# Operand sums of a two-layer network made earlier, stored in DRAM and loaded back

## The chip, the cores and the metric

The kernel runs on one core of a Trainium2 chip. The metric is the device time of one launch in microseconds (us). Before the change the median of three runs is 1302.47 us (1299.16 to 1303.53).

## The reference

Three layers follow each other. Attention through 32 packed queries per head gives x with 4608 tokens of 512 channels. A mixture of experts sends each token to one of 8 experts. A dense network with two matrices ends it:

```python
def _moe2_ref(x, w_in, w_out):        # x 4608 x 512, w_in 512 x 2048, w_out 2048 x 512
    h = x @ w_in
    g = h * (1.0 / (1.0 + np.exp(-h)))
    return (g @ w_out).astype(np.float32)
```

All is float32. The change concerns this last network, and the place in the expert stage where its weights are converted.

## The kernel before

The program has three parts: attention (0 to 280 us), the experts, called the middle stage here (`experts`, 280 to 516 us), and the dense network (`ffn`, 516 us to the end). The part `ffn` again has two phases.

**Seven products in place of eight.** Both matrix products cut each operand into 2 by 2 corners and use seven corner products (a Strassen scheme, `terms`): A11 B11, A12 B21, S4 B22, A22 T4, S1 T1, S2 T2, S3 T3. S1 to S4 are sums of activation corners, T1 to T4 sums of weight corners. Every operand is held as a high part (rounded to `fp32r`, a ScalarE cast) and a low part (source minus high part, a subtraction); three matmuls make one precise product.

**Middle stage.** `conv` turns 32 blocks of the 64-bit weights into float32 with six VectorE instructions each, and `conv_store` writes them to `wf_d`.

**Phase 1** computes silu(x @ w_in) in 40 calls of `group(z, g)`: z is one of five blocks of tokens (the last, z = 4, is half as wide), g one of eight blocks of W_in. The first eight groups have z = 0; the other 32 follow the list `order`, and position i below is an index into it. A group is seven times six matmuls (`Pm`, lines 844 to 846). It drains its PSUM banks a, b, c, d with VectorE sums and ScalarE silus into a ring of tiles `cs`, stored to `c_d[z]` as four corners 0 to 3 (C11, C12, C21, C22). The seventh product of a group is issued inside the next one. Other work (weight operands, activation sums, corners of W_out) is queued with `later` and issued in four places of a group (`hook`), each with a budget in nanoseconds. `operand(g, x)` builds the 14 parts of W_in block g into one of four tiles TT[0..3]; blocks 4 to 7 are built twice. `corner_steps` and `build4` split W_out; blocks 5 to 7 go to `v_d` and are loaded back by `slice_load` into TT[1..3], since those tiles still hold W_in until phase 1 ends.

**Phase 2** works through 18 units (z, 128 columns of each corner), four for z = 0 to 3 and two for z = 4. A unit has seven products in the order 1, 7, 6, 2, 5, 3, 4, each of eight pairs of matmuls (lines 1081 and 1082). For each product `split` casts 128x1024 values on ScalarE (line 1059) and subtracts on VectorE, two products ahead. `drain` empties PSUM; GpSimd adds two halves (`both`) and SyncE writes the output. `load_unit` fetches the four corners of the next unit. Their sums are made on GpSimd, four instructions of 128x1024 a unit: E1 = C21 + C22 and C21 = C11 - C21 (`early_sums`, in `split` of product 5), C11 = E1 - C11 (after product 1's split), C12 = C12 - C11 (after product 2's):

```python
        if i == 1:
            tt(POOL, c11, E1, c11, ALU.subtract)
        elif i == 2:
            tt(POOL, c12, c12, c11, ALU.subtract)
        elif i == 5 and 0 < u < len(units) - 1:
            early_sums(u + 1)
```

Every engine runs its instructions in program order. SyncE (SP) issues all DMAs here, also in order: an issue that waits holds up those behind it. `tt` records every VectorE and GpSimd sum of `ffn` under line 837.

## Time and profile before

| | |
|---|---|
| median of 3 runs | 1302.47 us |
| profiled execution | 1308.87 us, of which the span of its instructions is 1307.1 us |
| TensorE (PE) busy | 1210.1 us, 93% of the span |
| VectorE (DVE) busy | 831.9 us, 64% |
| ScalarE (ACT) busy | 542.1 us, 41% |
| GpSimd (POOL) busy | 477.0 us, 36% |
| moved by DMA | 235.71 MB |
| mean granted TensorE clock | 0.983 |

TensorE is the busiest engine. The stretches in which it isn't busy are short and spread over the second half of the span, so the profile is read by stage: 280 to 516 us the middle stage, 516 to 867 us phase 1 as far as its last three narrow groups, 867 to 932 us the passage to phase 2, 932 to 1286 us the units of phase 2.

### The profile page before, as it was taken

Reading aid. Unit: us, or ns where it says so; the run is one execution under the profiler, and the core shown is the slowest. Engines: PE = TensorE matmul, PEld = TensorE weight load, DVE = VectorE, ACT = ScalarE, POOL = GpSimd, SP = SyncE. Lnnn points to the kernel's source line nnn. Section 1 sums busy time; section 2 is a strip of 40 time slices with the busy share of each in tenths; the row PEclk is TensorE's granted clock in tenths of the full one; section 3 lists DMA queues with packets and bytes.
Section 4 is the critical chain, followed back from the end, with each engine's and each line's share of the span. In section 5 each row is a group of like instructions: output and inputs, shape, how many; then the busy total and the mean of one; then the engine's idle time right before and its main releaser. Section 6 shows DMA issues by size and latency. Waiting matters only on the chain. (4 is left out here: it accounts for less than half of the span.)

```text
span 1307.1 us, 23467 instructions
## 1 busy us (share of the span) xinstructions
PE 1210.1 (93%) x9008; PEld 1042.3 (80%) x9009; DVE 831.9 (64%) x1323; ACT 542.1 (41%) x925; POOL 477.0 (36%) x430
## 2 busy tenths in 40 slices
PE   6999989999999999999999999997899999999997
PEld 4777668999999999777788778876677787778876
DVE  2566557678886765785563566644667666666664
ACT  2666652334233314654453445543333333333342
POOL 2233210000000001761252313422876767676865
PEclk9999999999999999999999999997999999999999
DMA  6897738567976564634346544788435353525351
GB/s 190 243 256 219 239 103 296 195 219 254 333 235 233 165 209 129 209 133 161 135 153 220 191 129 160 254 294 287 125 97 145 97 145 97 145 81 157 85 160 34
DMA packets 237686, 235.71 MB, mean 180 GB/s; under 512 B 34168, under 2 KB 185208, under 8 KB 237440
## 3 DMA queue, kind: packets, MB, share of 16 engines
q1 hardware_dynamic: 231040, 229.44, 55.9%
q10 hardware_dynamic: 6528, 4.72, 1.2%
q8 instruction: 72, 1.18, 0.4%
q14 instruction: 46, 0.38, 0.1%
HBM read 155.60 MB, written 78.51 MB: 179 GB/s over the span
## 5 line engine op out<-in xcount | busy, mean ns | idle before, releaser
L837 DVE TENSOR_TENSOR x<-p,x 128x512 f32<-128x512 f32 (+1 forms) x171 | 109.2, 649 | 94.1 <-POOL raw L837 40.8
L876 ACT ACTIVATE x<-x 128x512 f32<-128x512 f32 (+1 forms) x114 | 67.9, 598 | 144.9 <-DVE x L837 133.3
L1081 PE MATMUL p<-x,e 128*128 128x512 f32 x315 | 118.2, 402 | 2.7 <-DMA x<-v_d 2.7
L601 PE MATMUL ps<-hkm,w2s 128*128 128x288 f32 x384 | 114.5, 298 | 0.9 <-DVE yb L612 0.9
L603 PE MATMUL ps<-hkm,w2s 128*128 128x288 f32 x384 | 113.5, 296 | 1.4 <-DVE w2s L574 1.4
L305 POOL TENSOR_TENSOR cu<-co,co 128x256 f32<-128x256 f32 x1 | 0.7, 729 | 284.7 <-PEq L682 284.7
L602 PE MATMUL ps<-hqm,w2s 128*128 128x288 f32 x320 | 94.2, 294 | 0.0
L1082 PE MATMUL p<-x,x 128*128 128x256 f32 x320 | 91.9, 287 | 0.0
L837 DVE TENSOR_TENSOR x<-p,y 128x512 f32<-128x512 f32 (+1 forms) x75 | 50.1, 668 | 44.5 <-PE p L846 40.4
L601 PEld LDWEIGHTS ps<-hkm,w2s 128*128 128x128 f32 x384 | 72.1, 188 | 7.6 <-DVE hqm L537 5.0
L1081 PEld LDWEIGHTS p<-x,e 128*128 128x128 f32 x315 | 60.0, 191 | 17.0 <-DMA x<-v_d 3.1
L603 PEld LDWEIGHTS ps<-hkm,w2s 128*128 128x128 f32 x384 | 72.0, 188 | 1.9 <-DVE w2s L574 1.8
L837 POOL TENSOR_TENSOR raw<-x 128x256 f32<-128x256 f32 x72 | 69.6, 981 | 8.3 <-DVE x L837 6.0
L528 PE MATMUL ps<-at,mh 128*128 128x288 f32 x224 | 66.8, 298 | 3.0 <-PEq L682 3.0
L837 POOL TENSOR_TENSOR raww1c<-raww1c 128x1024 f32<-128x1024 f32 x18 | 56.9, 3160 | 30.4 <-issue 29.7
L530 PE MATMUL ps<-at,mh 128*128 128x288 f32 x224 | 66.8, 298 | 0.0
L529 PE MATMUL ps<-at,mh 128*128 128x288 f32 x224 | 66.7, 298 | 0.0
L1059 ACT CAST e<-rawe 128x1024 fp32r<-128x1024 f32 x27 | 28.3, 1049 | 91.7 <-POOL rawe L837 91.7
L837 POOL TENSOR_TENSOR rawe<-rawe 128x1024 f32<-128x1024 f32 x18 | 57.8, 3213 | 20.8 <-issue 20.1
L1082 PEld LDWEIGHTS p<-x,x 128*128 128x128 f32 x320 | 62.7, 196 | 0.0
L533 ACT ACTIVATE hkm<-ps 128x576 fp32r<-128x576 f32 x42 | 27.4, 653 | 84.1 <-PE ps L530 83.9
L573 ACT CAST w2s<-w2c 128x1024 fp32r<-128x1024 f32 x32 | 33.8, 1055 | 66.4 <-PE ps L602 42.0
(423 smaller groups left out, 3895.4 us busy)
## 6 DMA issues: line engine op xcount, KB each, us to landing
c_d<-x SPq DMA_DIRECT2D x128, 256.0 KB, 2.0
raww1c<-c_d SPq DMA_DIRECT2D x36, 512.0 KB, 7.2
rawe<-c_d SPq DMA_DIRECT2D x36, 512.0 KB, 6.4
w1c<-in_moe_w_dram SPq DMA_DIRECT2D x32, 512.0 KB, 7.1
w2c<-in_moe_w_dram SPq DMA_DIRECT2D x32, 512.0 KB, 6.6
y_d<-yb SPq DMA_DIRECT2D x36, 288.0 KB, 4.5
raw<-wf_d SPq DMA_DIRECT2D x38, 256.0 KB, 3.3
raw<-y_d SPq DMA_DIRECT2D x36, 256.0 KB, 4.6
```

Source lines behind the costliest of these rows:

```text
L528: PE.matmul(out=a[:, i, 0:H2], lhsT=mh[0][:, t, f], rhs=at[0][:, t, n], start=t == 0, stop=False)
L529: PE.matmul(out=a[:, i, 0:H2], lhsT=mh[0][:, t, f], rhs=at[1][:, t, n], start=False, stop=False)
L530: PE.matmul(out=a[:, i, 0:H2], lhsT=mh[1][:, t, f], rhs=at[0][:, t, n], start=False, stop=t == 1)
L573: ACT.copy(out=h, in_=w2c[c % 2])
L601: PE.matmul(out=a[:, i, 0:H2], lhsT=h[:, k, :], rhs=hT(0, k, n), start=k == 0, stop=False)
L602: PE.matmul(out=a[:, i, 0:H2], lhsT=h[:, k, :], rhs=hT(1, k, n), start=False, stop=False)
L603: PE.matmul(out=a[:, i, 0:H2], lhsT=l[:, k, :], rhs=hT(0, k, n), start=False, stop=k == 7)
L837: eng.tensor_tensor(out=o, in0=x, in1=y, op=op)
L876: ACT.activation(out=y, in_=x, func=ACTF.Silu)
L1059: ACT.copy(out=h, in_=src)
L1081: PE.matmul(out=o, lhsT=h[:, g], rhs=x, start=first and n == 0, stop=False, skip_group_check=True)
L1082: PE.matmul(out=o[:, 256:512], lhsT=l[:, g], rhs=x[:, 0:256], start=False, stop=n == G - 1, skip_group_check=True)
```

## The change

- Middle stage: after every second conversion GpSimd makes T1 to T4 of that block with four subtractions of 128x256, and SP stores them to `u_d` (16 blocks: eight of W_in, eight of W_out). `ffn` loads them into `x4` where it made them before, on GpSimd.
- Phase 1: the low parts that GpSimd made go to VectorE. For z above 0, a group also makes E1 = C21 + C22 and C21 = C11 - C21 with two VectorE instructions, and stores five tiles in place of four. The ring `cs` gets a seventh tile.
- W_in blocks 4 to 7 are stored to `t_d` after their first use (1.835 MB each, i = 0 to 3) and loaded back after i = 20, 21, 24 and 25, in place of a second build.
- Passage: the four tiles of W_out for `build4` are loaded at i = 27, before `load_unit(0)`; the fourth goes to `x4`. `build4` and `early_sums(0)` run on VectorE alone. `slice_load` of blocks 6 and 7 (TT[2], TT[3]) is one DMA each; block 5 comes last, and the first two products take it after the other seven.
- Phase 2: C11 and C12 sums on VectorE. For z above 0, `early_sums` is a load of E1. GpSimd keeps only `both`.

```diff
@@ experts: conv
+        if 7 < i < 16 or i >= 24:
...
+            for q, x, y in ((t1, b12, b11), (t2, b22, t1), (t3, b22, b12), (t4, b21, t2)):
+                POOL.tensor_tensor(out=q, in0=x, in1=y, op=ALU.subtract)
+            for n in range(2):
+                SP.dma_start(out=u_d[i - 8 if i < 16 else i - 16][:, 512 * n:512 * n + 512], in_=four[n])
@@ ffn: group
+                def f():
+                    e1 = ring()
+                    tt(DVE, e1, c21, kept[22])
+                    store(4, e1)
+                    tt(DVE, c21, kept[11], c21, ALU.subtract)
+                    store(2, c21)
+                return f
@@ ffn
+    def t_load(g, x):
+        held[g] = x
+        SP.dma_start(out=TT[x][:, 0:3584].bitcast(F32), in_=t_d[g].bitcast(F32))
@@ ffn: split, early_sums
         if i == 1:
-            tt(POOL, c11, E1, c11, ALU.subtract)
+            tt(DVE, c11, E1, c11, ALU.subtract)
         elif i == 2:
-            tt(POOL, c12, c12, c11, ALU.subtract)
+            tt(DVE, c12, c12, c11, ALU.subtract)
         elif i == 5 and 0 < u < len(units) - 1:
             early_sums(u + 1)
 
     def early_sums(u):
+        if units[u][0]:
+            load_unit(u, (4,))
+            return
         c11, c12, c21, c22 = raws[u % 2]
-        tt(POOL, E1, c21, c22)
-        tt(POOL, c21, c11, c21, ALU.subtract)
+        tt(DVE, E1, c21, c22)
+        tt(DVE, c21, c11, c21, ALU.subtract)
@@ ffn: the list order, from i = 16
-             (3, 0), (3, 1), (3, 2), (4, 0), (3, 3), (4, 1), (3, 4), ...
+             (3, 0), (3, 1), (3, 2), (4, 0), (4, 1), (3, 3), (3, 4), ...
+    next_t = {19: (4, 0), 20: (5, 1), 23: (6, 2), 24: (7, 3)}
...
+        if i < 4:
+            t_store(4 + i)
...
+        if i - 1 in next_t:
+            t_load(*next_t[i - 1])
@@ ffn: the first products of phase 2
+        if s < 2:
+            product(s, (0, 1, 2, 3, 4, 6, 7))
+            if s:
+                for x in range(2):
+                    product(x, (5,))
+                    drain(x)
```

VectorE in phase 2, from the end of one unit with z = 3 into the next, before (raww1c and rawe hold the corners of alternate units, x_7157 is E1, e, at, x_9864 and x_9995 are low parts, p are PSUM banks):

```order
L837 TENSOR_TENSOR at_135<-rawe_10060,at_134 128x1024
L837 TENSOR_TENSOR x_7158<-p_7162,x_7158 128x512
L837 TENSOR_TENSOR x_9864<-rawe_10060,e_3365 128x1024
L837 TENSOR_TENSOR x_7158<-p_7161,y_3367 128x512
L837 TENSOR_TENSOR x_9995<-rawe_10060,x_9995 128x1024
L837 TENSOR_TENSOR e_3365<-rawe_10060,e_3365 128x1024
L837 TENSOR_TENSOR at_135<-x_7157,at_134 128x1024
L837 TENSOR_TENSOR y_3367<-p_7164,y_3366 128x512
L837 TENSOR_TENSOR x_9864<-rawe_10060,e_3365 128x1024
L837 TENSOR_TENSOR x_9995<-rawe_10060,x_9995 128x1024
L837 TENSOR_TENSOR x_7158<-p_7164,y_3366 128x512
L837 TENSOR_TENSOR x_7158<-p_7165,x_7158 128x512
```

The same part of VectorE's program after the change (x_7259 is E1):

```order
L849 TENSOR_TENSOR at_141<-rawe_10108,at_140 128x1024
L849 TENSOR_TENSOR rawe_10108<-x_7259,rawe_10108 128x1024
L849 TENSOR_TENSOR x_7260<-p_7264,x_7260 128x512
L849 TENSOR_TENSOR x_9910<-rawe_10108,e_3371 128x1024
L849 TENSOR_TENSOR x_7260<-p_7263,y_3373 128x512
L849 TENSOR_TENSOR x_10044<-rawe_10108,x_10044 128x1024
L849 TENSOR_TENSOR e_3371<-rawe_10108,e_3371 128x1024
L849 TENSOR_TENSOR rawe_10108<-rawe_10108 128x1024
L849 TENSOR_TENSOR at_141<-x_7259,at_140 128x1024
L849 TENSOR_TENSOR y_3373<-p_7266,y_3372 128x512
L849 TENSOR_TENSOR x_9910<-rawe_10108,e_3371 128x1024
L849 TENSOR_TENSOR x_10044<-rawe_10108,x_10044 128x1024
```

Two instructions are new in a unit, the second and the eighth row: C11 and C12, which were on GpSimd.

SP in phase 2, one unit with z = 2, before (c_d_76 to 79 are the four corners):

```order
L1032 DMA raww1c<-c_d_76 128x8x128
L1032 DMA raww1c<-c_d_79 128x8x128
L1032 DMA raww1c<-c_d_78 128x8x128
L1032 DMA raww1c<-c_d_77 128x8x128
L1127 DMA out_dram<-raw 128x512 x2
```

And after (c_d_79 to 82 are the four corners, c_d_83 is E1):

```order
L1077 DMA raww1c<-c_d_79 128x8x128
L1077 DMA raww1c<-c_d_81 128x8x128
L1077 DMA raww1c<-c_d_82 128x8x128
L1077 DMA raww1c<-c_d_80 128x8x128
L1077 DMA x_7259<-c_d_83 128x8x128
L1175 DMA out_dram<-raw 128x512 x2
```

A fifth load stands behind the four, into the one tile of E1, and ahead of the two writes of the output.

## Rows read from the trace of the kernel before

**Rows 1.** Stretches: length, busy us of PE, PEld, DVE, ACT, POOL; PEclk, DMA, GB/s
```profile
280.00:516.00 236.00, 231.86 (x1822) 223.59 (x1821) 179.28 (x282) 80.30 (x114) 5.44 (x6) 0.99 0.68 222
340.00:360.00 20.00, 20.00 (x153) 20.00 (x152) 17.69 (x30) 6.28 (x10) 0.00 (x0) 1.00 0.93 318
516.00:867.00 351.00, 335.92 (x1559) 276.13 (x1558) 217.58 (x325) 167.88 (x344) 130.49 (x146) 1.00 0.52 181
867.00:932.00 65.00, 47.39 (x265) 41.56 (x265) 30.36 (x37) 25.43 (x41) 29.71 (x15) 0.87 0.74 234
932.00:1286.00 354.00, 329.38 (x1808) 280.96 (x1807) 225.93 (x194) 127.64 (x145) 253.90 (x130) 0.98 0.44 119
```
**Rows 2.** ScalarE in time: start, us, operation; one copy a group (L903), a unit (L1098)
```profile
661.42 0.59 ACT L903 COPY y<-p 128x512 f32<-128x512 f32 x1
670.94 0.59 ACT L903 COPY x<-p 128x512 f32<-128x512 f32 x1
...
931.58 0.58 ACT L1098 COPY y<-p 128x512 f32<-128x512 f32 x1
...
1285.66 0.58 ACT L1098 COPY y<-p 128x512 f32<-128x512 f32 x1
```
**Rows 3.** Chain of waits through one unit of phase 2: start, us, what
```profile
1023.40 7.08 DMA raww1c<-c_d
...
1030.64 2.79 POOL x L837
...
1038.18 2.35 POOL raww1c L837
...
1043.25 1.77 DVE x L837
...
1045.74 6.80 DMA rawe<-c_d
```
**Rows 4.** TensorE in phase 2, two matmuls eight pairs apart
```profile
957.19 0.39 PE L1081 MATMUL p<-x,e 128*128 128x512 f32 x1
...
959.97 0.39 PE L1081 MATMUL p<-x,x 128*128 128x512 f32 x1
```
**Rows 5.** VectorE in phase 2: start, us, operation, idle time before it
```profile
1023.90 1.22 DVE L837 TENSOR_TENSOR at<-x,at 128x1024 fp32r<-128x1024 f32 x1
1025.59 0.69 DVE L837 TENSOR_TENSOR y<-p,y 128x512 f32<-128x512 f32 x1 [0.47 <-PE p L1082]
...
1038.12 3.48 DVE L837 TENSOR_TENSOR at<-raww1c,at 128x1024 fp32r<-128x1024 f32 x1
```
**Rows 6.** GpSimd beside the last of these
```profile
1038.14 2.38 POOL L837 TENSOR_TENSOR raww1c<-x,raww1c 128x1024 f32<-128x1024 f32 x1
```
**Rows 7.** SP's issues of one unit's loads
```profile
1022.05 4.71 SPq L1032 DMA_DIRECT2D raww1c<-c_d  x4
```
**Rows 8.** Landing of the loads of phase 2: KB each, median us to landing
```profile
raww1c<-c_d SPq DMA_DIRECT2D x28, 512.0 KB, 7.2
```
**Rows 9.** TensorE in the passage, with idle time before and its releaser
```profile
888.32 0.58 PE L844 MATMUL p<-e,t 128*128 128x256 f32 x1 [7.40 <-DVE raw L837]
...
902.01 0.80 PE L1081 MATMUL p<-x,e 128*128 128x512 f32 x1 [2.73 <-DMA x<-v_d]
```
**Rows 10.** Chain of waits in the passage
```profile
871.65 7.48 DMA c_d<-x
...
879.15 4.80 DMA x<-wf_d
```
**Rows 11.** VectorE in the passage, a narrow drain
```profile
874.18 0.42 DVE L837 TENSOR_TENSOR x<-p,x 128x256 f32<-128x256 f32 x1
```
**Rows 12.** The page: a GpSimd subtraction of 128x256 (mean in ns after the busy time)
```profile
L305 POOL TENSOR_TENSOR cu<-co,co 128x256 f32<-128x256 f32 x1 | 0.7, 729 | 284.7 <-PEq L682 284.7
```
**Rows 13.** TensorE in the passage, narrow group: two matmuls eight trios apart
```profile
870.09 0.28 PE L844 MATMUL p<-e,t 128*128 128x256 f32 x1
...
872.97 0.28 PE L844 MATMUL p<-e,t 128*128 128x256 f32 x1
```

More of the change, by code (lines that the diff above doesn't have):

```diff
@@ L206, in build @@
             P = [ps.tile([128, 2, 512], F32, name=f"ps{i}") for i in range(4)]
[L207 removed]
+            experts(tc, s1, sums, R, P, first, ident, a2_d, y_d, g_d, pp_d, w1, w2, win, wout, wf_d, u_d)
         s2.close()
         with ExitStack() as s1:
[L210 removed]
+            ffn(tc, s1, sums, y_d, wf_d, t_d, c_d, u_d, v_d, out)
 class Early:
@@ L316, in both @@
                 x()
-        return [lambda: both(*steps, his[0], his[1]), *[lambda i=i: both(*his[i + 2:i + 3], los[i]) for i in range(6)]]
+        return [lambda: both(*(steps if fresh else ()), his[0], his[1]), *[lambda i=i: both(*his[i + 2:i + 3], los[i]) for i in range(6)]]
 class Fixed:
@@ L557, in experts @@
     raw = [T([128, 512], f"raw{i}") for i in range(4)]
+    four = sums.y3
     turn = [0]
@@ L807, in experts, with ffn @@
                 conv_store(x)
-def ffn(tc, st, sums, y_d, wf_d, c_d, u_d, v_d, out):
+def ffn(tc, st, sums, y_d, wf_d, t_d, c_d, u_d, v_d, out):
     nc = tc.nc
@@ L972, in ffn, with both_k, get @@
+    def both_k(z, now, then):
+        r0, r1 = {}, {}
+        def get(r, k, i):
+            r[i] = fetch(z, k, i)
+        for i in (3, 2, 0, 1):
+            get(r0, 0, i)
+        dead = {6: 3, 7: 2, 9: 0, 10: 1}
+        later(now, *steps(z, 0, r0, {m: (lambda i=i: get(r1, 1, i)) for m, i in dead.items()}))
+        later(then, *steps(z, 1, r1))
     win = dict(zip((1, 9), sums.next))
+    w = wf_d.bitcast(F32)
+    tmp = [x4[:, 256 * i:256 * i + 256] for i in range(4)]
+    ow = {}
     def win_load(g):
-        win[g], win[g + 8] = w_raw(g), w_raw(g + 8)
@@ L1135, in ffn @@
     X = [x1[i // 4][:, 512 * (i % 4):512 * (i % 4) + 512] for i in range(8)]
-    load(1, 0, X[0:4])
+    for i in range(4):
+        fetch(1, 0, i, X[i])
     todo = [*steps(1, 0, X[0:4]), *steps(1, 1, X[4:8])]
@@ L1142, in ffn @@
         if g == 2:
-            load(1, 1, X[4:8])
+            for i in range(4):
+                fetch(1, 1, i, X[4 + i])
         if g in (5, 6):
@@ new lines, in ffn @@
+            later(now + 4, *operand(i - 4, i - 4))
+        if i == 11:
+            both_k(3, now + 5, now + 10)
+        if i == 16:
+            k = [[fetch(4, k, j) for j in range(2)] for k in range(2)]
+            k = [{0: x[:, 0:256], 1: y[:, 0:256], 2: x[:, 256:512], 3: y[:, 256:512]} for x, y in k]
+            later(now + 4, *steps(4, 0, k[0]), *steps(4, 1, k[1]))
+        if i in (19, 21, 23, 25):
+            n = (i - 19) // 2
+            flush()
+            o_load(4 + n if n else 0)
+            later(now + 3, *corner_steps(4 + n if n else 0, slices(n - 1) if n else slice0))
@@ L1254, in ffn @@
+        if i == 27:
+            flush()
+            for x, y in (("B11", at[0]), ("T3", at[1]), ("T2", half(b, 3)), ("B21", x4)):
+                staged(x, y)
         if i == 28:
-            flush()
             raws[0] = quarters("w1c")
-            for x, y in (("B11", at[0]), ("T2", x4), ("T3", at[1])):
-                later(now + 1, (0, lambda x=x, y=y: staged(x, y)))
-            later(now + 1, (0, lambda: load_unit(0)))
+            load_unit(0)
         if i == 29:
-            later(now, (0, small))
@@ L1262, in ffn @@
-            later(now + 1, (0, lambda: staged("B21", x5[:, 0:1024])), b4("B11", DVE), b4("T2", DVE), b4("T3", POOL))
+            later(now + 1, (0, small))
+            later(now + 1, b4("B11"), b4("B21"), b4("T3"))
         if i == 30:
-            later(now, (0, lambda: early_sums(0)))
-            later(now + 1, (0, lambda: slice_load(1)), b4("B21", DVE), (0, lambda: split(0)))
+            later(now, (0, lambda: slice_load(1)))
+            later(now, b4("T2"), (0, lambda: early_sums(0)), (0, lambda: split(0)))
```

202 lines of the change are left out of this document (95 added, 107 removed).

## Prediction

> **What bounds the kernel now.** I read the busy time by stretch first, to see where TensorE isn't busy, then for each such stretch what it waits for. The middle stage has almost nothing to give: TensorE is busy 231.86 of 236 us [rows 1]. Phase 1 has 351 - 335.92 = 15 us of idle TensorE, the passage 65 - 47.39 = 17.6 us at a mean granted clock of 0.87, phase 2 354 - 329.38 = 24.6 us [rows 1]. Idle time is not all: in phase 2 the copy that opens a unit comes 16 times between 931.58 and 1285.66 us, so a unit takes 354.08 / 16 = 22.13 us [rows 2], while TensorE alone needs less: eight pairs take 959.97 - 957.19 = 2.78 us, seven products 19.5 us [rows 4]. So each unit lasts 2.6 us longer than its matmuls.
>
> The chain of waits says why [rows 3]. It goes through one unit in a loop that TensorE is hardly in: the load of the next corners (7.08 us), GpSimd's sums one behind the other (2.79 us for E1 and more until 1040.5), the last splits on VectorE (1.77 us), and then the tiles are free and the next load starts at 1045.74, 22.3 us after the one before. GpSimd is busy 253.90 of 354 us there [rows 1]. VectorE is drawn in: a low part of 128x1024 takes 1.22 us alone and 3.48 us beside a GpSimd sum of 2.38 us [rows 5, 6]. What bounds phase 2 is GpSimd's chain, not TensorE.
>
> **Phase 2, units 1 to 17.** For z above 0 the four GpSimd sums leave the loop: two are made in phase 1, two go to VectorE. VectorE's work in a unit is then seven low parts and two sums of 1.22 us and five drains of 0.69 us [rows 5], 14.4 us of 19.5. GpSimd keeps four additions of 128x256, 0.73 us each [rows 12]; if each held up VectorE in full that would be 2.9 us more, 17.3 us, still under TensorE. E1 is now waited for by VectorE, and behind that wait stand a drain and the next splits. Its tile is free when the fifth product's split is done, about 8 us into the unit; SP first issues four loads (4.71 us for the four [rows 7]) from about 2 us on, so E1 is issued at 8 to 9 us, and lands 7.2 us later [rows 8], at 15 to 16 us. It is first asked for beside the sixth product (13.9 + 1.2 = 15.1 us), and TensorE needs what stands behind it only at about 19. So the wait is covered, with 3 us to spare. I take 19.6 us a unit, next to the 19.5 of rows 4: (22.13 - 19.6) x 16 = 40 us. For z = 0 the sums stay, now on VectorE: in units 1 and 2 `early_sums` waits for loads that land 10 to 12 us into the unit and adds 2.4 us behind that; I give 1 us back in each, so the term is -38 us. Bounds: at 20.6 us a unit (329.38 us of busy TensorE over 16, which holds its slow stretches too [rows 1]) the gain is 24 us, at 19.5 us it is 43 us.
>
> **Passage, 867 to 932 us.** The longest wait of TensorE, 7.40 us [rows 9], comes from one tile: a store had to land (7.48 us) before it was free, then B21 was loaded into it (4.80 us) [rows 10], while VectorE stood behind its split. After a wait TensorE also runs slower: the mean granted clock of 0.87 over 65 us is 17 us at the lower of its two levels (1.2 for 2.4 GHz). With B21 loaded at i = 27 into another tile this wait goes. What is late next is VectorE, which now has GpSimd's share as well. From the first of the three narrow groups: 21 narrow sums of 0.42 us [rows 11], four `build4` subtractions, two early sums, and two splits with one sum behind them, nine of 1.22 us [rows 5]: 8.8 + 11.0 = 19.8 us, against three groups of 42 matmuls at 2.88 / 24 = 0.12 us [rows 13], 15.1 us. That is a stall of 4 to 5 us. Then the load of block 7 into TT[3] can be issued only after the last product of the second narrow group, and it is one DMA of 1.835 MB: at 342 GB/s (318 GB/s at a share of 0.93 [rows 1]) 5.4 us and some 2 us to land. SP reaches it some 2 us after that product (a silu and two sums feed the stores ahead of it), so it lands 9.4 us behind; TensorE has one narrow group (5.0 us) and six pairs (2.1 us) before it needs block 7. It is 2.3 us late, near the 2.73 us that TensorE waits for such a load now [rows 9]; I take 3. Two more us go to VectorE in the first unit, which holds the last three operands. TensorE's own work in the 65 us is about 41 us at full clock (47.39 less some 6 for the slow level); 41 + 5 + 3 + 2 + 1 = 52, a gain of 13 us. Bounds: 24 us with no stall, nothing if new waits of the same length take over.
>
> **Phase 1, 516 to 867 us.** Removed: GpSimd's low parts and sums, and the second build of four weight blocks. Added on VectorE: two sums in 32 groups (24 wide at 2 x 0.69, 8 narrow at 2 x 0.42, 40 us), 24 low parts of activations (18 wide, 6 narrow, 15 us), two low parts in each of 11 builds (9 us), less four builds (4 x (0.69 + 3 x 0.42) = 8 us): 56 us, so 217.58 + 56 = 274 of 351 us [rows 1, 5, 11], 78% where it was 62%, without counting that operations slowed by GpSimd become shorter. That fits under TensorE on the mean, not in every group: a wide group takes 9.52 us [rows 2], and seven sums and ten queued steps of 0.69 us would be 11.7 us. Such groups are few (i = 0, 12).
> The DMAs are the other cost. Groups i = 20 to 27 get four loads of 1.835 MB beside 2.75 MB for W_out, 5.5 MB of `v_d` and 7.9 MB of corners: 23.5 MB in 4 x 9.52 + 4 x 5.04 = 58.2 us, 403 GB/s, over the 342 GB/s that rows 1 bear out. That is 69 us of transfers, 10 us too long; the load of block 4 is also needed one group after its issue, 9.5 us against 7.5. Most of this is hidden, as stores have over a group to land before their tile is used again. The Trainium skill would put the excess at 7 us: "DMA: Bandwidth & Descriptors", section Specifications, gives about 358 GB/s of memory bandwidth a core, 65.5 us by an estimate from that. By rows 1, which are measured, it is 10. I take half of the 15 us of idle time as gone with GpSimd's contention, 7 us, and give 4 us back: -3 us. Bounds: -15 (no idle left) to +12 (the whole DMA excess, and 2 for block 4).
>
> **Middle stage.** 64 GpSimd subtractions of 0.73 us [rows 12], 47 us, on an engine that has 5.44 us of work there, 16 bursts of 2.9 us. VectorE has 179.28 of 236 us, but 17.69 of 20 us at 340 to 360 [rows 1]. Beside GpSimd it loses: of the 3.48 us in rows 5, 2.26 are over 1.22, nearly the 2.38 of GpSimd's instruction. If half of a burst falls on such operations, VectorE has 17.69 + 2 = 19.7 of 20 us: full, not over. Four PSUM banks and a slack stretch behind it hide that; I take +1 us, bounds 0 to +6. Here a rule speaks against the change: the Trainium skill ("SBUF — State Buffer", section SBUF: two separate sides) has GpSimd and a VectorE operation with two SBUF inputs lock each other out for a whole instruction. Rows 5 and 6 look like it. With every burst paid in full VectorE would need 17.69 + 4 = 21.7 of 20 us, over the dense 60 us about 5 us more, and the sum would stand 4 us higher.
>
> **Sum.** -38 - 13 - 3 + 1 = -53 us on the profiled execution's 1308.87 us. That execution is 0.5% over the median of 1302.47, so I take the difference over: about 1250 us. The likeliest case's own range is 1236 to 1266.
>
> **Rivals.** *E1 takes GpSimd's place.* If E1 lands 4 us later than the sum has it, VectorE stands, and TensorE loses 1 to 2 us a unit over 13 units, some 18 us: 1268 us. For it: five loads a unit in place of four, in pieces of 512 bytes, and E1 last in the queue. Against: DMA is at a share of 0.44 in phase 2 [rows 1].
> *Phase 1 becomes full.* VectorE's dense groups and the DMA excess are paid in full: +12 in place of -3, 1265 us. For it: 403 GB/s; against: the backlog starts empty and is spread over eight groups.
> *Slower.* Phase 1's transfers set its time. It moves 181 GB/s x 351 us = 63.5 MB [rows 1], and the change adds 7.3 MB of E1 and 14.7 MB of `t_d` (the rest nets out within 1 MB): 85.5 MB. If the mix of large blocks and small stores ran at the present mean of 181 GB/s, this would be 472 us in place of 351, and the kernel would be at 1250 + 121 = 1371 us. It decides from 85.5 MB / (351 + 53) us, 212 GB/s down, where the loss eats the gain. Against: 234 GB/s at a share of 0.74, 318 at 0.93 [rows 1].
> *No effect.* The loop has another link than GpSimd (landing and freeing of tiles), and the unit stays at 22 us: with the passage's gain lost as well, 1302 us.
>
> **How the numbers follow.** Forecast 0.65, E1 0.14, phase 1 0.11, slower 0.06, no effect 0.04. A change of up to 0.3% (4 us) is about what a measurement here can't tell from none. The first three are faster: 0.90; same 0.04; slower 0.06. The range 1234 to 1284 us takes the forecast with its bounds, and both weaker gains; what it leaves out is the last two cases and the tails of phase 1.
>
> **What would show it.** In the changed kernel's profile: 16 units of 19.5 to 19.9 us, GpSimd with four short additions a unit, VectorE's low parts at 1.22 us, and no wait of TensorE over 1 us for z above 0. In the passage, no wait of 7 us, and one of about 3 us for the load of TT[3]. In phase 1, TensorE idle for 8 to 18 us. Wrong would be: units over 20.6 us, with VectorE waiting for the load of E1; a phase 1 over 360 us with TensorE behind stores or t_d loads; a middle stage longer by more than 6 us.

## The result and the profile after

The changed kernel takes 1286.48 us (median of 4 runs, 1285.41 to 1287.27) against 1303.00 us for the kernel before on the same chip: a ratio of 0.9875, with a 95% interval of 0.9848 to 0.9902. It is faster by 16.5 us, where 53 were forecast; 1286.48 lies 2.5 us over the range. By the profiled executions the difference is 1307.1 - 1285.4 = 21.7 us of span, since the profiled execution of before (1308.87 us) lay 6 us above its median and that of after (1287.26) 0.8 us.

Four stretches of [rows 1], now in the changed kernel (same columns; phase 2 ends 7 us earlier, so its row is shorter):
```profile
280.00:516.00 236.00, 226.65 (x1769) 218.25 (x1754) 183.09 (x276) 78.17 (x112) 48.92 (x56) 0.99 0.75 248
516.00:867.00 351.00, 338.78 (x1582) 280.11 (x1581) 235.81 (x417) 159.33 (x319) 3.71 (x4) 1.00 0.68 240
867.00:932.00 65.00, 50.63 (x294) 44.27 (x293) 46.43 (x61) 28.08 (x44) 6.08 (x4) 0.95 0.79 254
932.00:1279.00 347.00, 335.33 (x1871) 290.19 (x1870) 240.02 (x237) 132.47 (x147) 94.11 (x67) 0.98 0.53 144
```
GpSimd (the fifth busy column) has left phases 1 and 2 as forecast: 130.49 us became 3.71, 253.90 became 94.11. But it came back in the middle stage (5.44 to 48.92 us), and there TensorE lost 5 us of busy time in the same 236 us.

Stretches by the clock tell it better than by windows. The middle stage here runs from the first expert matmul to the first FFN matmul, phase 1 to the copy that opens group i = 28, the passage from there to the first product of unit 1:

| us | before | after | difference | forecast |
|---|---|---|---|---|
| up to the first expert matmul | 198.5 | 195.8 | -2.7 | 0 |
| middle stage | 319.9 | 327.4 | +7.4 | +1 |
| phase 1 | 342.6 | 340.1 | -2.5 | -3 |
| passage | 63.1 | 61.9 | -1.2 | -13 |
| units 1 and 2 | 46.6 | 57.2 | +10.7 | -5.3 |
| units 3 to 17 | 330.5 | 296.9 | -33.7 | -32.7 |

(The forecast's -38 for phase 2 is split here: two units of 19.6 + 1 us in place of 46.6, and the rest. The first row differs by chance: it lies between 195.3 and 200.4 us in the 17 profiles of this study, whose kernels are alike up to there. The row of phase 1 owes something to chance too, as the part on why the prediction was right and wrong says.)

From unit 3 on the forecast stands. The copy that opens a unit, of units 4 and 17 (start, length, engine, line, operation, idle time before it and its releaser):
```profile
1005.21 0.59 ACT L1146 COPY y<-p 128x512 f32<-128x512 f32 x1 [3.02 <-PE p L1130]
...
1262.43 0.59 ACT L1146 COPY y<-p 128x512 f32<-128x512 f32 x1 [3.03 <-PE p L1130]
```
(1262.43 - 1005.21) / 13 = 19.79 us, against 22.13 in [rows 2]. TensorE waits for nothing in these units, and the low part beside GpSimd that took 3.48 us in [rows 5] is 1.2 us long. GpSimd's four additions take 1.40 us each on the mean, where the prediction took 0.73 from [rows 12]; TensorE does not feel it.

Units 1 and 2 are where it failed. First TensorE with its two long waits, then VectorE just before each:
```profile
944.91 0.77 PE L1129 MATMUL p<-mh,at 128*128 128x512 f32 x1 [7.44 <-DVE y L849]
...
971.30 0.76 PE L1129 MATMUL p<-mh,e 128*128 128x512 f32 x1 [4.23 <-DVE y L849]
```
```profile
941.68 1.23 DVE L849 TENSOR_TENSOR x<-raww1c 128x1024 f32<-128x1024 f32 x1 [6.95 <-DMA raww1c<-c_d]
942.94 1.22 DVE L849 TENSOR_TENSOR raww1c<-raww1c 128x1024 f32<-128x1024 f32 x1
944.08 0.68 DVE L849 TENSOR_TENSOR y<-p,y 128x512 f32<-128x512 f32 x1
...
967.66 1.22 DVE L849 TENSOR_TENSOR x<-rawe 128x1024 f32<-128x1024 f32 x1 [3.85 <-DMA rawe<-c_d]
...
970.48 0.68 DVE L849 TENSOR_TENSOR y<-p,y 128x512 f32<-128x512 f32 x1
```
Read the second fence: `y<-p,y` at 944.08 is u2, the drain of product 6 (the third of a unit) out of bank b. It needs nothing that is late, but it stands on VectorE behind the two sums of `early_sums`, and the first of these waits 6.95 us for the next unit's corners. TensorE's product 5 (the fifth of a unit) accumulates into the same bank b, so it waits for u2. SP issued these corners late, right behind two output writes:
```profile
929.54 2.09 SPq L1175 DMA_DIRECT2D out_dram<-raw  x2
931.73 6.17 SPq L1077 DMA_DIRECT2D raww1c<-c_d  x4
```
The two waits are 11.7 us, yet the units are 57.2 - 2 x 19.8 = 17.6 us too long. The rest is the clock behind the waits:
```profile
925.00:955.60 30.60, 22.74 (x115) 19.04 (x114) 20.29 (x20) 10.20 (x11) 6.14 (x5) 0.83 0.31 86
955.60:982.40 26.80, 22.57 (x115) 19.25 (x114) 17.10 (x17) 8.12 (x10) 6.75 (x5) 0.87 0.36 99
982.40:1002.20 19.80, 19.80 (x115) 17.16 (x114) 14.11 (x15) 8.12 (x9) 5.55 (x5) 1.00 0.59 160
```
The granted clock is 0.83 and 0.87 in these two units, and 1.00 in the next: the same 115 matmuls keep TensorE busy for 22.7 us in place of 19.8.

In the passage the wait of 7.40 us in [rows 9] is gone, and seven others stand there:
```profile
878.62 0.39 PE L856 MATMUL p<-e,t 128*128 128x256 f32 x1 [1.66 <-DVE y L849]
882.30 0.39 PE L856 MATMUL p<-e,t 128*128 128x256 f32 x1 [1.99 <-ACT y L928]
885.15 0.38 PE L856 MATMUL p<-e,t 128*128 128x256 f32 x1 [1.15 <-DVE y L849]
891.53 0.53 PE L856 MATMUL p<-e,t 128*128 128x256 f32 x1 [3.96 <-DVE raw L849]
898.06 0.39 PE L856 MATMUL p<-e,x 128*128 128x256 f32 x1 [0.45 <-DVE raw L849]
904.69 0.51 PE L1129 MATMUL p<-t,e 128*128 128x512 f32 x1 [3.53 <-DMA t<-v_d]
...
916.77 0.47 PE L1129 MATMUL p<-mh,e 128*128 128x512 f32 x1 [1.20 <-ACT x L1061]
```
They add up to 13.9 us. Before, the two of [rows 9] were 10.1 us, and with three shorter ones (1.26, 0.72 and 0.84 us) the waits were 13.0. So TensorE waits 1 us longer than before; what fell is its busy time, 47.9 us for 49.6, at a granted clock of 0.94 where it was 0.86. The wait of 3.96 us has a run of VectorE before it, in which unit 0's sums and first split stand ahead of a group's drain:
```profile
885.81 1.22 DVE L849 TENSOR_TENSOR x<-raww1c 128x1024 f32<-128x1024 f32 x1
887.06 1.23 DVE L849 TENSOR_TENSOR raww1c<-raww1c 128x1024 f32<-128x1024 f32 x1
888.21 1.22 DVE L849 TENSOR_TENSOR x<-raww1c,e 128x1024 fp32r<-128x1024 f32 x1
889.46 1.23 DVE L849 TENSOR_TENSOR raww1c<-x,raww1c 128x1024 f32<-128x1024 f32 x1
890.60 0.42 DVE L849 TENSOR_TENSOR x<-p,y 128x256 f32<-128x256 f32 x1
```

### The profile page after: what moved, and what is told of

Read it like the earlier page. It is cut to its first block, busy times and chain, and to the rows that moved or that the text cites. A ratio compares the mean times of both kernels' runs of the same rounds, so it can differ in the third digit from the quotient of the medians.

```text
span 1285.4 us, 23420 instructions
## 1 busy us (share of the span) xinstructions
PE 1201.5 (93%) x9008; PEld 1040.1 (81%) x9009; DVE 878.3 (68%) x1468; ACT 534.9 (42%) x901; POOL 214.1 (17%) x273
## 4 chain that ended last, share of the span: by engine, by line
PE 44%; DVE 8%; DMA 6%; issue 3%; ACT 2%; SPq 0%; DVEq 0%; POOLq 0%; POOL 0%; ACTq 0%
PE p L1129 17%; PE p L1130 8%; PE p L856 5%; PE p L858 5%; PE p L857 5%; DVE x L849 4%; DMA c_d<-x 1%; DMA x<-u_d 1%; DMA v_d<-e 1%; DVE raw L849 1%; DVE e L849 1%; PE ps L605 1%; PE ps L603 1%; PE ps L604 1%; DMA raww1c<-c_d 1%
## 5 line engine op out<-in xcount | busy, mean ns | idle before, releaser
L849 POOL TENSOR_TENSOR raw<-x 128x256 f32<-128x256 f32 x72 | 100.9, 1402 | 650.1 <-DMA rawe<-c_d 387.9
L889 ACT ACTIVATE x<-x 128x512 f32<-128x512 f32 (+1 forms) x113 | 67.3, 600 | 131.4 <-DVE x L849 126.2
L849 DVE TENSOR_TENSOR x<-p,y 128x512 f32<-128x512 f32 (+1 forms) x75 | 49.6, 662 | 36.9 <-PE p L858 26.2
L575 ACT CAST w2s<-w2c 128x1024 fp32r<-128x1024 f32 x32 | 33.7, 1054 | 67.2 <-PE ps L604 36.6
L1129 PE MATMUL p<-x,x 128*128 128x512 f32 x160 | 60.5, 404 | 0.0
L604 PEld LDWEIGHTS ps<-hqm,w2s 128*128 128x128 f32 x320 | 60.0, 188 | 0.0
L1129 PE MATMUL p<-x,at 128*128 128x512 f32 x155 | 58.6, 405 | 0.0
L604 PE MATMUL ps<-hvm,w2s 128*128 128x288 f32 x192 | 56.6, 295 | 0.0
## 6 DMA issues: line engine op xcount, KB each, us to landing
vm<-in_v_dram SPq DMA_DIRECT2D x8, 1024.0 KB, 10.7
```

What stands on the lines that cost most here:

```text
L604: PE.matmul(out=a[:, i, 0:H2], lhsT=h[:, k, :], rhs=hT(1, k, n), start=False, stop=False)
L849: eng.tensor_tensor(out=o, in0=x, in1=y, op=op)
L889: ACT.activation(out=y, in_=x, func=ACTF.Silu)
L1129: PE.matmul(out=o, lhsT=h[:, g], rhs=x, start=first and g == 0, stop=False, skip_group_check=True)
```

## The experiments

All variants in one table, in us. "i 20 to u1" is from the copy of group i = 20 to unit 1's first product; "unit" is the mean of units 4 to 16. Base A is the changed kernel, base S is `sums_after_drain`. Each ratio is to the kernel before, timed on the same chip. A median is of four runs, of six for `combined` and of two for the last two rows; the stretches are of one profile each.

| kernel (base) | median | ratio, 95% interval | middle | phase 1 from its first copy | i 20 to u1 | units 1, 2 | unit |
|---|---|---|---|---|---|---|---|
| before | 1303.00 | | 319.9 | 340.9 | 128.5 | 46.6 | 22.06 |
| after | 1286.48 | 0.9875, 0.9848 to 0.9902 | 327.4 | 338.4 | 129.4 | 57.2 | 19.79 |
| z0_premade (A) | 1278.56 | 0.9801, 0.9762 to 0.9841 | 326.6 | 350.6 | 129.6 | 39.9 | 19.79 |
| sums_after_drain (A) | 1275.32 | 0.9770, 0.9725 to 0.9814 | 327.0 | 340.6 | 130.5 | 40.5 | 19.79 |
| the same again | 1273.15 | 0.9770, 0.9720 to 0.9820 | 327.1 | 343.7 | 134.3 | 41.0 | 19.41 |
| no_block_loads (A) | 1283.96 | 0.9843, 0.9807 to 0.9880 | 325.9 | 334.3 | 125.7 | 57.1 | 19.79 |
| mid_no_sums (A) | 1282.03 | 0.9846, 0.9787 to 0.9905 | 317.7 | 343.8 | 133.4 | 57.1 | 19.79 |
| mid_dummy_sums (A) | 1281.98 | 0.9844, 0.9788 to 0.9899 | 324.5 | 341.6 | 131.5 | 56.6 | 19.41 |
| mid_sums_dve (S) | 1273.60 | 0.9764, 0.9698 to 0.9830 | 326.6 | 340.5 | 132.2 | 40.8 | 19.79 |
| tail_on_pool (S) | 1278.66 | 0.9808, 0.9758 to 0.9859 | 326.7 | 342.7 | 136.8 | 39.8 | 19.41 |
| late_7 (S) | 1277.09 | 0.9783, 0.9728 to 0.9838 | 328.5 | 341.4 | 132.4 | 40.5 | 19.79 |
| weights_phase1 (S) | 1275.88 | 0.9772, 0.9721 to 0.9823 | 317.3 | 352.0 | 138.0 | 40.0 | 19.41 |
| unit0_premade (S) | 1273.25 | 0.9758, 0.9703 to 0.9812 | 324.4 | 342.6 | 131.4 | 40.6 | 19.79 |
| no_slice_loads (S) | 1271.91 | 0.9711, 0.9656 to 0.9765 | 330.8 | 342.2 | 127.9 | 40.9 | 19.79 |
| combined (S) | 1277.50 | 0.9774, 0.9732 to 0.9817 | 319.6 | 352.6 | 132.2 | 40.6 | 19.79 |
| no_slice_work (S) | 1263.50 | 0.9688, 0.9647 to 0.9730 | 324.9 | 336.2 | 129.8 | 39.6 | 19.41 |
| no_slice_dma (S) | 1262.58 | 0.9681, 0.9639 to 0.9723 | 325.6 | 337.7 | 124.9 | 40.5 | 19.79 |

How much a stretch differs by itself can be read from kernels that are alike in it: the middle stage takes 324.4 to 330.8 us in the 11 profiles with GpSimd's 64 sums of weights, mean 326.8, and "i 20 to u1" 129.4 to 134.3 us, mean 131.9, in the six that are alike there (after, S twice, the three mid kernels).

### Units 1 and 2: the order on VectorE

`z0_premade` makes z = 0 like the other z:
```diff
-                if not z:
-                    store(2, c21)
-                    return lambda: None
...
-        c11, c12, c21, c22 = raws[u % 2]
-        tt(DVE, E1, c21, c22)
-        tt(DVE, c21, c11, c21, ALU.subtract)
+        load_unit(u, (4,))
```


> E1 and C11 - C21 made in phase 1 for z = 0 too, so early_sums only loads in every unit. Theory (u2 of the sixth product stands on VectorE behind early_sums' wait for the corners, and the fifth product needs that PSUM bank): units 1 and 2 fall from 30.4 and 26.8 us to 19.8 us each, no TensorE wait over 1 us in them, and VectorE's run of 885.8 to 890.6 us in the passage loses two sums (2.45 us); 16 to 20 us less than the changed kernel, 1267 to 1271 us. Rival (the loads of the first units simply land late, behind the passage's transfers): units 1 and 2 stay over 24 us, 1281 us or more. Cost expected in phase 1: 16 more sums on VectorE and 2.1 MB more stores in the first eight groups, 0 to 3 us.

`sums_after_drain` does the same work and changes only the order:
```diff
-        elif i == 5 and 0 < u < len(units) - 1:
+        elif i == 5 and 2 < u < len(units) - 1:
             early_sums(u + 1)
...
-        if s == 5:
-            early_sums(1)
+        if u < 3 and i == order3[5]:
+            early_sums(u + 1)
```


> The same work as the changed kernel, but in units 1 and 2 VectorE gets early_sums three products later, behind the drains of the sixth and second product. Theory (order on VectorE before a PSUM bank): the TensorE waits of 7.4 and 4.2 us before the fifth product go, the units fall to 20 to 22 us, 9 to 14 us less than the changed kernel, 1272 to 1277 us. Rival (VectorE is too full in these units, or the loads are too late for any order): the waits come back at the next unit's first split, as 10 us of stall at another product, 1284 us or more.

Both take units 1 and 2 to 40 us, so the theory holds and its rival, late loads, falls: with the same loads at the same places and only VectorE's order changed, 16.7 of the 17.6 us are back. In `sums_after_drain` the copies that open units 1, 2 and 3 stand 19.92 and 19.60 us apart:
```profile
934.26 0.59 ACT L1146 COPY y<-p 128x512 f32<-128x512 f32 x1 [0.49 <-PE p L1130]
954.18 0.59 ACT L1146 COPY y<-p 128x512 f32<-128x512 f32 x1 [0.57 <-PE p L1130]
...
973.78 0.59 ACT L1146 COPY y<-p 128x512 f32<-128x512 f32 x1 [0.49 <-PE p L1130]
```
`sums_after_drain` beats both kernels: its interval of the ratio lies wholly under that of the changed kernel. Its medians are 11 and 13 us lower, not 16.7, since other stretches came out longer: in the first profile the part up to the first expert matmul, the same in both kernels, by 4.5 us (200.4 for 195.8) and phase 1 by 2.3. `z0_premade` was expected at 1267 to 1271 us and missed by 8: with its 16 more sums and 2.1 MB more stores phase 1 is 12 us longer, 6 of these in the first eight groups, where VectorE is busy 65.65 of 83.48 us (56.90 of 77.13 in `sums_after_drain`). Which of the two, sums or stores, costs it was not tried.

### The middle stage: GpSimd beside VectorE

`mid_no_sums` leaves GpSimd's subtractions out and stores the raw weights in their place:
```diff
-            for q, x, y in ((t1, b12, b11), (t2, b22, t1), (t3, b22, b12), (t4, b21, t2)):
-                POOL.tensor_tensor(out=q, in0=x, in1=y, op=ALU.subtract)
...
...
-                SP.dma_start(out=u_d[i - 8 if i < 16 else i - 16][:, 512 * n:512 * n + 512], in_=four[n])
+                SP.dma_start(out=u_d[i - 8 if i < 16 else i - 16][:, 512 * n:512 * n + 512], in_=(o, p)[n])
```


> GpSimd's 64 subtractions in the middle stage left out, the 8.4 MB of stores kept (raw weights are stored in place of the sums). Theory (VectorE is held up while GpSimd works): the first FFN group starts 4 to 5 us earlier, at 518 to 519 us in place of 523.2, and 1281 to 1283 us in all. Rival (the stores, their issue on SP, or the DMA traffic delay the middle stage): the first FFN group stays at 522 to 524 us and the time within 1.5 us of the changed kernel's.

`mid_dummy_sums` gives GpSimd its subtractions back, on tiles that nobody else uses:
```diff
+            POOL.tensor_tensor(out=t4[:, 0:1], in0=p[:, 0:1], in1=p[:, 1:2], op=ALU.subtract)
+            for q, x, y in ((t1, t4, t1), (t2, t1, t2), (t3, t2, t3), (t4, t3, t4)):
+                POOL.tensor_tensor(out=q, in0=x, in1=y, op=ALU.subtract)
```


> The kernel of mid_no_sums (raw weights stored in place of the sums), to which GpSimd's 64 subtractions are given back on a scratch tile of its own: after one element read from the converted weights they touch nothing that another engine or a store waits for. The middle stage lasts 327.4 us in the changed kernel, 317.7 us without the sums. Theory (VectorE is held up while a GpSimd instruction runs): 325 to 328 us. Rival (the sums hold the converted tiles, or the stores behind the sums hold their tile, and the next conversion waits): 317 to 319 us.

First expert matmul and first FFN matmul of `mid_no_sums`, then of `mid_dummy_sums`:
```profile
197.64 0.40 PE L603 MATMUL ps<-hkm,w2s 128*128 128x288 f32 x1
...
515.33 0.47 PE L854 MATMUL p<-mh,ta 128*128 128x512 f32 x1 [0.94 <-DVE yb L614]
```
```profile
195.99 0.40 PE L603 MATMUL ps<-hkm,w2s 128*128 128x288 f32 x1
...
520.53 0.47 PE L859 MATMUL p<-mh,ta 128*128 128x512 f32 x1 [0.94 <-DVE yb L614]
```
317.7 us without the sums, twice the gain that was expected, and 324.5 with sums that wait for nothing and hold nothing: most of the 9 us comes from GpSimd merely working. The rest, up to 3 us, may be the tiles that the real sums hold, but that is within the spread. The stores cost nothing: with them and without sums the stage is no longer than before (319.9). The total of `mid_no_sums` shows only 4.5 us of this; in its profile groups 20 to 28 take 73.1 us, the most of the six alike kernels, and in that of the changed kernel 67.6, the least. Where VectorE pays is in the groups by line (busy us, mean ns of one, idle time before): a low part and the first two steps of the weights' conversion, in the changed kernel (280 to 516 us) and then in `mid_no_sums` (280 to 510 us, the same counts):
```profile
L576 DVE TENSOR_TENSOR w2s<-w2c,w2s 128x1024 fp32r<-128x1024 f32 x23 | 29.3, 1274 | 2.3 <-ACT w2s L575 2.3
...
L654 DVE TENSOR_SCALAR cg<-cin 128x512 int32<-128x512 int32 x25 | 14.7, 587 | 10.2 <-DMA cin<-in_moe_w_in_dram 6.4 <-DMA cin<-in_moe_w_out_dram 3.8
L655 DVE TENSOR_SCALAR cu<-cin 128x512 int32<-128x512 int32 x25 | 13.7, 549 | 0.0
```
```profile
L576 DVE TENSOR_TENSOR w2s<-w2c,w2s 128x1024 fp32r<-128x1024 f32 x23 | 28.0, 1219 | 2.5 <-ACT w2s L575 2.5
...
L654 DVE TENSOR_SCALAR cg<-cin 128x512 int32<-128x512 int32 x25 | 10.6, 423 | 13.9 <-DMA cin<-in_moe_w_in_dram 8.5 <-DMA cin<-in_moe_w_out_dram 5.4
L655 DVE TENSOR_SCALAR cu<-cin 128x512 int32<-128x512 int32 x25 | 10.6, 422 | 0.0
```
The conversion's first two steps, which come while GpSimd sums the weights converted just before, grow from 423 to 587 ns and from 422 to 549 ns; with the low part that is 8.5 us. They read one tile from SBUF, not two. The Trainium skill ("SBUF — State Buffer", section SBUF: two separate sides) names both kinds, those with two SBUF inputs and those in a mode that takes two ports, as locked out while a GpSimd instruction runs. That both kinds of rows grow here agrees with it; in which mode the one-input steps run is shown by no run.

`mid_sums_dve` puts the sums on VectorE:
```diff
-                POOL.tensor_tensor(out=q, in0=x, in1=y, op=ALU.subtract)
+                DVE.tensor_tensor(out=q, in0=x, in1=y, op=ALU.subtract)
```


> On top of sums_after_drain (1275.3 us, middle stage 327.1 us) the middle stage's 64 subtractions go from GpSimd to VectorE, 0.42 us each, 27 us more for an engine that has 211 of 280 us of work there without them. Theory (GpSimd's 47 us of instructions cost VectorE most of their length): the middle stage falls to 319 to 323 us. Rival (VectorE is near full in its dense stretches, so work on it costs as much as being locked out): 325 to 332 us.

326.6 us: neither better nor worse. 27 us of work in VectorE's own queue cost the stage what 57 us of GpSimd beside it cost (64 sums of 0.89 us; the prediction had 0.73).

`weights_phase1` undoes this part of the change: no sums in the middle stage, fresh ones by GpSimd in phase 1.
```diff
-        return list(zip((0, 690, 425, 425, 425, 425, 425), sums.weights(TT[x], win.pop(g), win.pop(g + 8), tmp, fresh)))
+        return list(zip((0, 690, 425, 425, 425, 425, 425), sums.weights(TT[x], win.pop(g), win.pop(g + 8), tmp, True)))
...
+        if i in (9, 10, 11, 12):
+            products_load(i - 8)
+            later(now + 3, (0, lambda i=i: products(i - 8)))
```


> On top of sums_after_drain (1275.3 us; middle stage 327 us; phase 1, first group to group 28, 340.7 us): the weight sums of the middle stage undone, made by GpSimd in phase 1 as in the kernel before (W_in operands from freshly made sums, W_out sums of blocks 1 to 4 stored in groups 9 to 12, the others as they are needed). Theory (the middle stage is bound by TensorE and VectorE's dense stretches, phase 1 has slack): the middle stage falls to 317 to 320 us, phase 1 gains 0 to 4 us, 1266 to 1272 us. Rival (VectorE is held up by GpSimd in phase 1 as much as in the middle stage): phase 1 is 6 to 10 us longer, 1273 to 1278 us.

The middle stage fell to 317.3 us and phase 1 rose by 11 us, against the rival's 6 to 10: the rival, and more. The first eight groups, in `sums_after_drain` and in `weights_phase1` (columns of [rows 1]):
```profile
529.12:606.25 77.13, 76.04 (x332) 61.60 (x331) 56.90 (x103) 44.90 (x95) 3.71 (x4) 1.00 0.65 215
```
```profile
517.50:600.87 83.37, 78.04 (x332) 61.10 (x331) 63.93 (x103) 44.80 (x96) 25.15 (x28) 1.00 0.49 170
```
VectorE does the same 103 operations in 63.93 us in place of 56.90, and the stretch is 6.2 us longer. So moving the weight sums from phase 1 to the middle stage is worth nothing by itself in this kernel: 10 us in one place for 11 in the other.

### Groups 20 to 31 and the passage

Seven kernels look for what holds this stretch. `no_block_loads` drops `t_store` and `t_load`:
```diff
-        SP.dma_start(out=TT[x][:, 0:3584].bitcast(F32), in_=t_d[g].bitcast(F32))
...
-            t_store(4 + i)
```


> The four W_in operand blocks are neither stored nor loaded back (14.7 MB less traffic); the products of blocks 4 to 7 for z = 3, 4 then run with the operands of blocks 0 to 3. Theory (transfers: groups i = 16 to 28 lose 3.4 us to full DMA queues, and the passage inherits the backlog): those groups regain 3 to 4 us, and the passage from i = 28 to the first product another 3 to 6 us; 1276 to 1281 us. Rival (the passage is lost to VectorE's pile-up): the groups regain 3 us or less and the passage stays at 35 to 36 us; 1283 to 1286 us.

Phase 1 is 4 us shorter as the theory had it, all of it from group 16 on, but the passage behind is not (62.2 us), and the median of 1284 us is the rival's. Over both, "i 20 to u1" is 125.7 us, 4 under the changed kernel's and 6 under the mean of 131.9.

`tail_on_pool` and `unit0_premade` take sums from VectorE in the passage, by GpSimd or by making them earlier:
```diff
-                    tt(DVE, e1, c21, kept[22])
+                    E = POOL if tail else DVE
+                    tt(E, e1, c21, kept[22])
...
-        tt(DVE, E1, c21, c22)
-        tt(DVE, c21, c11, c21, ALU.subtract)
+        tt(DVE if u else POOL, E1, c21, c22)
+        tt(DVE if u else POOL, c21, c11, c21, ALU.subtract)
```


> On top of sums_after_drain: the E1 and C11 - C21 sums of the last three groups, and unit 0's two early sums and its C11 update, go from VectorE to GpSimd (the passage of sums_after_drain, from group 28 to unit 1, is 60.5 us). Theory (the passage is lost to VectorE's pile-up of 1.22 us and 0.42 us sums ahead of the drains): 3 to 6 us shorter, as in z0_premade, where two of these sums less gave 57.4 us. Rival (GpSimd holds VectorE up for as long as it works, and the sums are longer there): 59 to 64 us.

```diff
                 if not z:
+                    e1 = ring()[:, 0:128]
+                    tt(DVE, e1, c21[:, 0:128], kept[22][:, 0:128])
+                    SP.dma_start(out=c_d[z][4][:, g, 0:128], in_=e1)
+                    tt(DVE, c21[:, 0:128], kept[11][:, 0:128], c21[:, 0:128], ALU.subtract)
                     store(2, c21)
```


> On top of sums_after_drain: E1 and C11 - C21 of unit 0 alone (128 of 512 columns) made in the eight groups of z = 0, so that VectorE has no early sums in the passage. Theory (in the passage VectorE's 1.22 us sums stand ahead of the drains): the passage from group 28 to unit 1 falls from 60.5 to 55.5 to 57.5 us as in z0_premade (57.4 us), and the first eight groups lose 0 to 3 us where z0_premade lost 7; 1271 to 1275 us. Rival (z0_premade's shorter passage came from its longer groups 24 to 28, in which transfers drained): 59.5 us or more.

GpSimd made it 5 us worse (136.8; its passage of 64.8 us lies over even the rival's range), the early sums changed nothing (131.4; the passage itself 59.8 us, as the rival had it). In `unit0_premade` the wait of 3.96 us is gone, and the stretch is no shorter: VectorE's run is a wait that shows, not what sets the length.

`late_7` moves block 7 to the end of the first two products:
```diff
-            product(s, (0, 1, 2, 3, 4, 6, 7))
+            product(s, (0, 1, 2, 3, 4, 6))
...
-                    product(x, (5,))
+                    product(x, (7, 5))
```


> On top of sums_after_drain: the first two products leave block 7 to the end, behind twelve pairs of matmuls in place of six. Theory (the 3.4 us wait is for the landing of block 7's operands, issued after the second last group): the wait falls by 2.1 us, to 1.0 to 1.6 us, and the passage from group 28 to unit 1 to 58 to 59 us. Rival (what stands behind the wait, the last three operands and the splits on VectorE, is late anyway): the wait only moves to the next product, and the passage stays at 60 to 61 us.

The rival again, with a passage of 61.9 us. TensorE's wait for block 7 is 0.36 us, behind it stands one for the next load, and unit 0 takes 25.9 us where it took 26.3:
```profile
910.79 0.50 PE L1129 MATMUL p<-t,e 128*128 128x512 f32 x1 [0.36 <-DMA t<-v_d]
913.22 0.50 PE L1129 MATMUL p<-x,e 128*128 128x512 f32 x1 [1.81 <-DMA x<-v_d]
```
`no_slice_loads` leaves out the loads of the three slices. Of the other two, `no_slice_work` leaves out the building of the W_out operands of blocks 0 and 5 to 7 and keeps the transfers, `no_slice_dma` keeps the building and leaves out stores and loads:
```diff
-    slice_load(0, 0)
-    slice_load(0, 1)
...
-            slice_load(0, 2)
...
-            later(now, (0, lambda: slice_load(1)))
...
-            later(now + 1, (0, lambda: slice_load(2)), (0, lambda: begin(1)), (0, lambda: split(1)))
+            later(now + 1, (0, lambda: begin(1)), (0, lambda: split(1)))
```


> On top of sums_after_drain: the three stored W_out slices (5.5 MB) are not loaded, so blocks 5 to 7 of phase 2 run with what is left in their tiles. Theory (the passage is bound by transfers that can start only when a tile comes free): the 3.4 us wait goes and unit 0 with it, and the passage from group 28 to unit 1 falls from 60.5 to 52 to 55 us. Rival (VectorE's order holds it): only the 3.4 us wait goes, 57 to 58 us, since unit 0's other waits stay.

```diff
-            if i:
-                put(two(d)[:, :, 0:256], two(d)[:, :, 256:512], two(src), eng)
-            else:
-                put(d[:, 0:256], d[:, 256:512], src, eng)
             if done:
```


> On top of sums_after_drain: the W_out operands of blocks 0 and 5 to 7 are not built (12 ScalarE copies and 12 VectorE low parts of up to 1.22 us and 4 shorter ones less in groups 19 to 28, 16 operands in all); the loads, the stores to v_d and the slice loads stay. From group 24 to unit 1 is 94.6 us in sums_after_drain and 94 to 96 us in the kernel before and in nearly every variant. Theory (that stretch is bound by transfers, 29.6 MB at a share of 0.93): 93 to 96 us. Rival (VectorE's and ScalarE's pile-up): 85 to 90 us.

```diff
-            return t[:, 0:b - a], lambda d: SP.dma_start(out=v_d[n][:, a:b].bitcast(F32), in_=d.bitcast(F32))
+            return t[:, 0:b - a], None
```


> On top of sums_after_drain: the same W_out operands are built, but neither stored nor loaded back (11 MB less traffic); blocks 5 to 7 of phase 2 run with what is left in their tiles. Theory (bound by transfers): from group 24 to unit 1 84 to 88 us in place of 94.6, below the 90.2 us of no_slice_loads, and groups 16 to 24 1 to 3 us shorter. Rival (only block 7's 3.4 us wait hangs on transfers, the rest on VectorE and ScalarE): 90 to 91 us, as without the loads alone.

From i = 20 to unit 1: 127.9 us without the loads, 124.9 without loads and stores, 129.8 without the work, against 131.9 on the mean. From group 24 alone these are 90.2, 90.1 and 97.9 us, where the six alike kernels have 94.6 to 97.5. So from there the loads of the slices count for 5 to 6 us (the passage of `no_slice_loads`, 56.4 us, lies between its theory and its rival), and the missing work counts for nothing: the rival of `no_slice_work` falls. The rival of `no_slice_dma` is met, so the stores are not shown to count: the 3 us between it and `no_slice_loads` lie in groups 20 to 24, which differ by 4 us among the six alike kernels (34.2 to 38.4). What the missing work gave in those groups (4 us) was lost again in the passage, 63.3 us long at a granted clock of 0.84. Columns as in [rows 1], `no_slice_work` and then `no_slice_dma`:
```profile
830.00:870.00 40.00, 36.52 (x184) 29.77 (x183) 17.48 (x31) 10.52 (x22) 0.00 (x0) 1.00 1.03 373
870.00:925.00 55.00, 44.05 (x237) 39.11 (x236) 38.31 (x52) 23.43 (x38) 2.75 (x2) 0.81 0.83 264
```
```profile
830.00:870.00 40.00, 36.88 (x191) 31.50 (x192) 21.67 (x40) 14.24 (x29) 0.00 (x0) 1.00 0.93 306
870.00:925.00 55.00, 45.23 (x270) 40.08 (x269) 44.26 (x57) 26.10 (x41) 5.69 (x4) 0.94 0.46 147
```
So of all that was tried only fewer transfers shorten this stretch: by about 6 us for the blocks, by 4 to 7 for the slices, one profile each. That the two add up was not tried. One thing works against any single wait: in the six alike kernels TensorE's waits in the passage add up to between 10.9 and 13.9 us, its granted clock lies between 0.86 and 0.97, and yet the passage takes 60.3 to 62.4 us; the two with the fewest waits (10.9 and 11.0 us) have the lowest clock. Even without the slices TensorE loses time there: from i = 20 on five wide groups of 9.52 us, seven narrow ones of 5.04 and unit 0 at 19.5 would be 102.4 us. Those 22 us were not taken apart; 15 are waits, most of them for ScalarE and VectorE around the narrow groups.

### The versions together, and one again

`combined` has the edits of `sums_after_drain`, `weights_phase1` and `unit0_premade`.

> sums_after_drain, weights_phase1 and unit0_premade together. If the three theories hold, the gains add: 1262 to 1269 us. Rival (GpSimd's sums in the first groups and the extra sums of z = 0 on VectorE collide, and phase 1 gives back what the middle stage and the passage gain): 1273 us or more.

1277.5 us: the rival. The middle stage gained 7.5 us and phase 1 lost 12. So the three gains do not add. The second run of `sums_after_drain`:

> The kernel of sums_after_drain once more. Eight pairs of matmuls take 2.83 us (units of 19.79 us) in seven of the profiles of phase 2, 2.77 us (units of 19.41 us) in three others with the same instructions there. Theory (this differs from one execution to the next): units of 19.41 or 19.79 us, one pace throughout, and a median of 1269 to 1280 us. Rival (it belongs to the program): 19.79 us again.

Eight pairs of TensorE in phase 2, in the first profile of that kernel and in the second:
```profile
1099.91 0.40 PE L1129 MATMUL p<-t,e 128*128 128x512 f32 x1
...
1102.74 0.40 PE L1129 MATMUL p<-t,at 128*128 128x512 f32 x1
```
```profile
1099.93 0.39 PE L1129 MATMUL p<-x,e 128*128 128x512 f32 x1
...
1102.70 0.39 PE L1129 MATMUL p<-x,at 128*128 128x512 f32 x1
```
2.83 and 2.77 us at a granted clock of 1.00 in both: the pace is not the program's, and the theory holds. It is worth 0.38 us a unit, some 6 us in all, so medians of four runs that lie 3 us apart, as those of `sums_after_drain`, `mid_sums_dve` and `unit0_premade` do, are not told apart here.

## Why the prediction was right and wrong

Direction and mechanism of the main term were right. "What bounds phase 2 is GpSimd's chain" is shown by units 3 to 17: -33.7 us for a forecast of -32.7, and 19.79 us a unit for 19.6 (19.41 in executions of the faster pace). VectorE waits for E1 twice, 0.97 and 0.27 us, and TensorE does not feel it. Phase 1's -2.5 us for -3 is in part luck: from its first copy phase 1 takes 338.4 us here, the least of the nine profiles that are alike up to i = 28 (mean 341.6, up to 343.8), against 340.9 in the one profile of before. Its parts have the right direction: up to group 20 4.7 us were gained, where the forecast had 7, and from there to i = 28 2.1 us were lost, 5.5 on the mean of the nine, where 4 were given back; without the block loads that part is 4 us shorter than here.

Three steps failed, together 34 us: -53 + 34 is -19, and with the 2.7 us by chance ahead of the middle stage that is the -21.7 of the profiled executions.

*"in units 1 and 2 `early_sums` waits for loads that land 10 to 12 us into the unit and adds 2.4 us behind that; I give 1 us back in each."* It cost 17.6 us in place of 2. For E1 the prediction asked what stands behind the wait on VectorE; for these two units it stopped at the wait's own length. Behind it stood u2, and behind u2 the PSUM bank of the next product but one. The load also landed later than 12 us into the unit: SP issued it behind two output writes, and it was there at 941.68, 16.5 us after the start of unit 1. And the clock behind the waits took another 6 us. `sums_after_drain` gives 16.7 of the 17.6 us back by order alone.

*Passage, "41 + 5 + 3 + 2 + 1 = 52, a gain of 13 us".* The wait of 7.40 us went, block 7's wait came out as forecast (3.53 us for 3), and yet the passage is only 1 us shorter. Two terms were too small. The waits, 5 + 3 + 2 = 10 us, are 13.9. And the 41 us are TensorE's work at full clock, with at most the last 1 us for a lower one, where the granted clock is 0.94 over the passage: 0.06 x 61.9 = 3.7 us, an estimate. That is 7 of the 12 us; the rest stays open. The step also treated the stalls as separate and additive in a stretch where transfers run at shares of 0.9 and more most of the time: take one wait away and the next load is late (`late_7`), take the sums away and the length stays (`unit0_premade`). `no_block_loads` and `no_slice_dma` are what moves groups 20 to 31 and the passage together. The prediction had seen the backlog, and had put its price into phase 1.

*Middle stage, "I take +1 us, bounds 0 to +6".* It is +7.4, and 8 to 9 against kernels without these sums (mean of the three without: 318.2 us, of the eleven with: 326.8). GpSimd's sums took 57 us where 47 were forecast, and VectorE's 401 operations of the stage are busy for 249.4 us, against 238.0 in `mid_no_sums`. The assumption that half of a burst falls on something that VectorE can absorb was too kind; the rule weighed there, every burst paid in full, gave +5 and was the nearer one.

The rivals: E1 in GpSimd's place did not come; phase 1 as a full stage did not come in phase 1, but what it was built on, the transfers, costs 4 to 6 us from group 20 on, as `no_block_loads` shows. No rival had the order on VectorE in units 1 and 2, the largest single miss.
